# Regrouping the matmul stages of a retention and adapter kernel by the shape of the TensorE array

## The chip, the cores and the metric

The kernel runs on one core of a Trainium2 chip. The metric is the device time of one execution in microseconds; before the change it is the median of seven runs.

## What is computed

```python
B, H, S, D_ = q.shape                      # 8, 8, 576, 64, float32
scores = scale * np.matmul(q, k.transpose(0, 1, 3, 2))
gamma = 1.0 - 2.0 ** (-5.0 - np.arange(H))
Dmat = np.where(rel >= 0, gamma[:, None, None] ** rel[None, :, :], 0.0)
x = np.matmul(scores * Dmat[None], v)      # retention, per batch and head
x = x.transpose(0, 2, 1, 3).reshape(B * S, H * D_)     # 4608 x 512
logits = x @ w_gate                        # 8 experts
topk = np.argpartition(-logits, 2, axis=1)[:, :2]
w = softmax of the two chosen logits
out = x + sum over the two chosen e of w * ((x @ A[e]) @ B[e])     # A: 512x16, B: 16x512
```

The first half is a causal attention without softmax, with a decay by head. The second routes each of the 4608 rows to two of eight low-rank adapters.

## The kernel before, in words

**Units.** The sequence of 576 is cut into four chunks of 128 and one of 64. A unit is one chunk of two batches. A quad is the four batches (two units) that are loaded together; there are two quads in a chunk. So units 0 to 15 are full (unit t has chunk t // 4), and 16 and 17 are half units, which hold 64 positions of four batches each. A state P for every unit of a chunk (t % 4) carries what earlier chunks contribute; chunk 0 has none.

**Stages.** Every unit passes the stages below. In brackets stands the array shape, rows*columns, that its matmuls take in a full unit, as the profile prints it.

- T: q and k are transposed on TensorE, 16 transposes for each of qT and kT [64*128], and copied from PSUM to SBUF, by ScalarE or VectorE (two copies each, `g` = 0 and 1).
- S: scores, for batch 0 and then batch 1 (the halves `bs`) [64*128]; VectorE multiplies by the decay mask on the way out (`rt`, two for each half; `rh` in half units).
- Q: what the state contributes, written to `px` [64*64]. Chunk 0 takes the banks and issues nothing.
- U: the state's update, from k scaled by decay and v [128*64]. `scale_k` (GpSimd, line 261) scales k in place after k has been transposed and before U. VectorE adds (`pn`), GpSimd multiplies (line 395).
- R: scores times v, accumulated on `px` [128*64]; VectorE makes `xT` of each batch.
- Z: logits and the adapters' first product from `xT` [128*128] into `pz`; VectorE takes the two largest logits. V is ScalarE's sigmoid for the weights; W, on VectorE, makes the weighted `zc` and gives up the bank of `pz`.
- B: `xT` is transposed back into `po` [64*128], two banks.
- X: `zc` is transposed [128*128], ScalarE copies it to `zT`.
- Y: the adapters' second product is accumulated on `po` [128*128]; `po` is copied to `osb` by ScalarE, or with `spread` half by VectorE, and SP issues two output DMAs.

Half units take 64*64 for S, Q and R.

**What sets the order.** The order of stages is written out by hand (lines 608 to 708). `mm`, `vec` and `act` (lines 80 to 87) chain every instruction of an engine behind the one before, so each engine executes strictly in the order of the text; all their instructions show lines 81, 84 and 87 in the profile, and are told apart by the names of tiles. SP, too, issues its DMAs in the order of the text: `issue(n)` loads q, k and v of quad n, two quads ahead, into one of three buffers, and waits until that buffer has been read.

**PSUM.** `bank` (line 102) takes the first of a list of the eight banks and `done` (line 109) puts banks back at its end. This list is worked through while the program is built. On the chip, the first matmul into a bank waits for whoever last read it.

```python
    def bank(shape, name, dtype=FP32):
        n = free.pop(0)
        x = pp.tile(shape, dtype, tag=f"bank{n}", name=name)
        held[id(x)] = n, x
        return x
    def done(*tiles):
        free.extend(held.pop(id(x))[0] for x in tiles)
```

T and each half of S take two banks and put them back at once, in the list; B takes two and Y puts them back; Q takes two and R puts them back; Z takes one and W puts it back; U and X take one.

**The steady order** for a full unit t (lines 668 to 684): S(t, half 0), V(t-1), T(t+1, qT), S(t, half 1), W(t-1), T(t+1, kT), B(t-1), Q(t), U(t), scale_k(t+1), R(t), X(t-1), Z(t), Y(t-1). Each unit thus passes the four shapes once. Units 0 to 3 and the last three stand in orders of their own. Before unit 15's U, the Q of unit 16 is done too.

## Time and profile before

| | |
|---|---|
| median of seven runs | 195.27 us (193.52 to 195.41) |
| the profiled execution | 195.21 us |
| its span, first to last instruction | 193.5 us |
| TensorE clock granted, mean | 0.992 |
| ScalarE busy | 72.0 us (37%) |
| GpSimd busy | 59.0 us (31%) |
| HBM read, written | 28.91 MB, 9.44 MB |

Busy time of an engine is a union of its instructions. Matmuls are pipelined: one that is shown with 0.27 us may be followed by another 0.05 us later, so the start of a group and the start of the next tell how long it held TensorE, and its busy time does not. The profile's part 2 cuts the span into 40 slices of 4.84 us, with a digit for the busy tenths. In a timeline a line is a group of like instructions: start, busy time, engine, line, operation, tile written and tiles read, array shape for TensorE, shape of the operand, number, and in brackets the idle time before it with what ended it.

### The profile page before, as it was taken

The numbers are of one execution on the slowest core, as the hardware profiler recorded it, in microseconds if no ns is written. First come the engines' busy times: TensorE is split into PE (matmuls) and PEld (weight loads), VectorE is DVE, ScalarE is ACT, GpSimd is POOL, SyncE is SP. The second block draws the span as 40 slices with busy tenths as digits, with TensorE's granted clock in tenths as the row PEclk, the third lists the DMA queues.
The fourth block names the chain that finished last, engine by engine and source line by source line (L and its number), as shares of the span: only waits on it lengthen the run. The fifth ranks groups of instructions, "written<-read, shape, count | busy, mean of one in ns | idle before, by whom it ended". The sixth has DMA issues, their size and how long they took to land. (4 is left out here: it accounts for less than half of the span.)

```text
span 193.5 us, 8113 instructions
## 1 busy us (share of the span) xinstructions
PE 181.5 (94%) x3612; PEld 163.8 (85%) x3612; DVE 110.4 (57%) x281; ACT 72.0 (37%) x195; POOL 59.0 (31%) x70
## 2 busy tenths in 40 slices
PE   7899997999999999999998999999999999988870
PEld 2499997989999899999997999999999999977750
DVE  4467956575656474746564464646464746453650
ACT  4111164262526070707060525343444434070440
POOL 8985026040424233242415050514242420200000
PEclk9999999999999999999999999999999999999996
DMA  6999898797888598899869848999970302020243
GB/s 143 272 224 256 240 267 236 223 311 221 238 278 278 157 283 303 223 251 362 241 192 282 266 156 247 311 223 246 205 196 0 114 3 112 3 112 3 112 108 108
DMA packets 53746, 38.73 MB, mean 200 GB/s; under 512 B 27472, under 2 KB 49104, under 8 KB 53712
## 3 DMA queue, kind: packets, MB, share of 16 engines
q1 hardware_dynamic: 52736, 37.75, 69.4%
q8 instruction: 28, 0.46, 0.9%
q10 hardware_dynamic: 832, 0.34, 0.7%
q0 software_dynamic: 144, 0.13, 0.4%
q14 instruction: 6, 0.05, 0.1%
HBM read 28.91 MB, written 9.44 MB: 198 GB/s over the span
## 5 line engine op out<-in xcount | busy, mean ns | idle before, releaser
L261 POOL TENSOR_TENSOR k<-k,pack 128x512 f32<-128x512 f32 x32 | 32.7, 1042 | 81.2 <-PE pkT L81 70.6
L84 DVE TENSOR_TENSOR rt<-ps,mask 128x512 f32<-128x512 f32 x64 | 41.0, 686 | 16.5 <-PE ps L81 15.9
L81 PE MATMUL pz<-AW,xT 128*128 128x136 f32 x288 | 37.7, 283 | 0.3 <-DVE xT L84 0.2
L81 PE MATMUL ps<-qT,kT 64*128 64x128 f32 x512 | 35.7, 281 | 0.9 <-DVE kT L84 0.9
L81 PEld LDWEIGHTS pz<-AW,xT 128*128 128x128 f32 x288 | 34.7, 190 | 0.9 <-DVE xT L84 0.5
L81 PEld LDWEIGHTS ps<-qT,kT 64*128 64x128 f32 x512 | 31.0, 188 | 4.0 <-PE po L81 2.7
L81 PE MATMUL px<-rt,v 128*64 128x128 f32 x512 | 31.1, 273 | 0.7 <-issue 0.7
L87 ACT COPY osb<-po 128x256 f32<-128x256 f32 x68 | 20.6, 386 | 28.7 <-PE po L81 26.6
L84 DVE TENSOR_TENSOR xT<-px,asc 128x512 f32<-128x512 f32 x36 | 24.6, 691 | 9.0 <-PE px L81 8.0
L81 PEld LDWEIGHTS px<-rt,v 128*64 128x64 f32 x512 | 28.0, 137 | 0.8 <-issue 0.8
L87 ACT COPY zT<-pzt 128x256 f16<-128x256 f16 (+1 forms) x19 | 6.9, 361 | 53.9 <-PE pzt L81 53.9
L87 ACT COPY kT<-pkT 128x512 f32<-128x512 f32 x33 | 17.9, 590 | 14.7 <-PE pkT L81 14.7
L395 POOL TENSOR_TENSOR P<-pn,gdec 128x512 f32<-128x512 f32 x12 | 15.3, 1273 | 25.5 <-DVE pn L84 22.6
L87 ACT COPY qT<-pqT 128x512 f32<-128x512 f32 x32 | 17.2, 590 | 8.3 <-PE pqT L81 8.3
L81 PE MATMUL pu<-v,k 128*64 128x64 f32 x512 | 18.4, 225 | 1.6 <-POOL k L261 1.1
L81 PEld LDWEIGHTS pu<-v,k 128*64 128x64 f32 x512 | 16.3, 138 | 4.1 <-issue 2.6
L84 DVE COPY lg<-pz 128x16 f32<-128x16 f32 (+1 forms) x19 | 3.3, 173 | 26.4 <-PE pz L81 26.4
L84 DVE TENSOR_TENSOR pn<-pu,P 128x512 f32<-128x512 f32 x12 | 8.3, 692 | 16.0 <-PE pu L81 16.0
L81 PE MATMUL px<-qT,P 64*64 64x128 f32 (+1 forms) x512 | 15.9, 262 | 0.8 <-issue 0.7
L81 PEld LDWEIGHTS px<-qT,P 64*64 64x64 f32 x512 | 12.7, 133 | 1.8 <-issue 0.9
L81 PE MATMUL po<-id,xT 64*128 64x64 f32 x288 | 12.6, 224 | 0.7 <-DVE zc L84 0.7
L81 PE MATMUL pkT<-id,k 64*128 64x64 f32 x288 | 12.3, 223 | 0.1
(51 smaller groups left out, 150.8 us busy)
## 6 DMA issues: line engine op xcount, KB each, us to landing
out_dram<-osb SPq DMA_DIRECT2D x32, 256.0 KB, 3.1
q<-in_q_dram SPq DMA_DIRECT2D x4, 512.0 KB, 6.4
k<-in_k_dram SPq DMA_DIRECT2D x4, 512.0 KB, 7.1
v<-in_v_dram SPq DMA_DIRECT2D x4, 512.0 KB, 7.1
out_dram<-osb SPq DMA_DIRECT2D x6, 128.0 KB, 2.3
Arow<-in_moe_A_dram SPq DMA_DIRECT2D x1, 256.0 KB, 5.3
out_dram<-osb ACTq DMA_DIRECT2D x2, 128.0 KB, 2.7
Bcat<-in_moe_B_dram POOLq DMA_DIRECT2D x1, 128.0 KB, 5.1
```

The source lines that it names most:

```text
L81: chain("pe", nc.tensor.matmul(*args, **kw))
L84: chain("dve", getattr(nc.vector, fn)(**kw))
L87: chain("act", getattr(nc.scalar, fn)(**kw))
L261: gp.tensor_tensor(out=kk[:, b], in0=kk[:, b], in1=gv[:, 0].unsqueeze(2).broadcast_to((128, H, Dh)), op=ALU.mult,)
L395: nc.gpsimd.tensor_tensor(out=Pt, in0=pn, in1=gdec, op=ALU.mult)
```

## The change

The order of the stages is written anew. From unit 4 on, two units of a quad go through a loop together, and a stage of the one stands beside the same stage of the other. In the loop for t and t+1 the units of the quad before (t-2, t-1) pass Z, V and W, and those of the quad before that (t-4, t-3) pass B, X and Y. Six such loops (t = 4, 6, ... 14) are followed by a part written out for the half units. In the first part, units 2 and 3 pass S, U and R together.

With it go these edits:

- `stage_T` has a parameter `shared`; where it is set, the `g` = 1 copy is VectorE's. For unit 0 kT is copied batch by batch.
- `xT` has eight buffers instead of six, `zc` four instead of three.
- In chunk 0 U stands before Q, so U takes its bank first.
- V(1) stands before Y(0).
- Units 16 and 17 are transposed inside the loop of t = 14, between Q and U.

```diff
+    def stage_T(t, names=("qT", "kT"), shared=False):
...
+                if t == 0 and nm == "kT":
+                    for b in range(2):
+                        x = dst[:, b, :, rows(g)]
+                        if g == 1:
+                            vec("tensor_copy", out=x, in_=ps[g][:, :, b])
+                        else:
+                            act("copy", out=x, in_=ps[g][:, :, b])
+                elif t < 2 and nm == "qT" or shared and g == 1:
                     vec("tensor_copy", out=o, in_=ps[g])
                 else:
                     act("copy", out=o, in_=ps[g])
...
+            stage_U(0)
             stage_Q(0)
             stage_R(0)
             stage_T(1, ("qT",))
+            stage_T(1, ("kT",), shared=True)
             scale_k(1)
             stage_Z(0)
             stage_S(1)
             stage_W(0)
+            stage_U(1)
             stage_Q(1)
             stage_R(1)
             stage_T(2, ("qT",))
             stage_B(0)
             stage_X(0)
             stage_Z(1)
+            stage_V(1)
             stage_Y(0, spread=True)
+            stage_T(2, ("kT",), shared=True)
+            stage_T(3)
             scale_k(2)
+            scale_k(3)
+            stage_S(2)
+            stage_W(1)
+            stage_S(3)
+            for u in (2, 3):
+                stage_U(u)
+                stage_Q(u)
+                stage_R(u)
...
+        if t < 4 or units[t][2] or not is_full(t):
             continue
+        done_, near = [u for u in (t - 4, t - 3) if u > 0], (t - 2, t - 1)
+        here = (t, t + 1)
+        for nm in ("kT", "qT"):
+            stage_T(t, (nm,), shared=True)
+        scale_k(t)
+        for u in done_:
+            stage_B(u)
+        stage_T(t + 1, ("kT",))
+        scale_k(t + 1)
+        stage_S(t, (0,))
+        stage_T(t + 1, ("qT",))
+        stage_S(t, (1,))
+        stage_S(t + 1)
+        for u in done_:
+            stage_X(u)
+        stage_Z(near[0])
+        stage_V(near[0])
+        for u in done_:
+            stage_Y(u)
+        stage_Z(near[1])
+        stage_V(near[1])
+        if units[t][0] > 0:
+            for u in here:
+                stage_Q(u)
+        for u in near:
+            stage_W(u)
+        if t + 2 == NU - 2:
+            stage_T(t + 2)
+            stage_T(t + 3)
+        for u in here:
+            stage_U(u)
+            if units[t][0] == 0:
+                stage_Q(u)
+            stage_R(u)
+    h, n = NU - 2, NU - 1
+    stage_S(h); stage_Q(h); stage_B(h - 4); stage_B(h - 3); stage_X(h - 4); stage_X(h - 3)
+    stage_Z(h - 2); stage_V(h - 2); stage_Y(h - 4, spread=True); stage_Y(h - 3, spread=True)
+    stage_W(h - 2); stage_S(n); stage_R(h); stage_Z(h - 1); stage_V(h - 1); stage_Q(n)
+    stage_W(h - 1); stage_B(h - 2); stage_B(h - 1); stage_X(h - 2); stage_X(h - 1)
+    stage_Z(h); stage_V(h); stage_Y(h - 2, spread=True); stage_Y(h - 1, spread=True)
+    stage_R(n); stage_W(h); stage_B(h); stage_X(h)
+    for g in range(2):
+        stage_Z(n, (g,)); stage_W(n, (g,))
+    stage_Y(h); stage_B(n)
+    for g in range(2):
+        stage_X(n, (g,)); stage_Y(n, (g,), spread=True, last=True)
```

(The last part has one call on each line in the file; it is set closer here.)

## The prediction, before the result was known

> **What bounds the kernel now.** I read the page's shares first, then its slices, then the timeline of one unit in the steady part.

> ```profile
> PE 181.5 (94%) x3612; PEld 163.8 (85%) x3612; DVE 110.4 (57%) x281; ACT 72.0 (37%) x195; POOL 59.0 (31%) x70
> ...
> PE   7899997999999999999998999999999999988870
> ```

> TensorE is full from slice 7 to slice 34; VectorE, the next engine, is busy 57% of the span. So what TensorE does between 30 and 170 us is the time, and a new wait there costs its full length.

> The timeline of TensorE (start, busy, tile, array shape rows*columns); I read starts only, from group to group:

> ```profile
> 130.97 0.65 PE L81 MATMUL pkT<-id,k 64*128 64x64 f32 x16
> 131.46 0.67 PE L81 MATMUL po<-id,xT 64*128 64x64 f32 x16
> 132.06 1.10 PE L81 MATMUL px<-qT,P 64*64 64x128 f32 x32
> 133.09 1.15 PE L81 MATMUL pu<-v,k 128*64 128x64 f32 x32
> 134.07 1.92 PE L81 MATMUL px<-rt,v 128*64 128x128 f32 x32
> 135.93 0.29 PE L81 MATMUL pzt<-ident,zc 128*128 128x128 f16 x2
> 136.05 2.07 PE L81 MATMUL pz<-AW,xT 128*128 128x136 f32 x16
> 137.96 0.60 PE L81 MATMUL po<-Bcat,zT 128*128 128x256 f16 x4
> 138.49 1.16 PE L81 MATMUL ps<-qT,kT 64*128 64x128 f32 x16
> 139.48 0.66 PE L81 MATMUL pqT<-id,q 64*128 64x64 f32 x16
> 139.98 1.11 PE L81 MATMUL ps<-qT,kT 64*128 64x128 f32 x16
> 140.93 0.65 PE L81 MATMUL pkT<-id,k 64*128 64x64 f32 x16
> ```

> One unit takes 9.95 us (139.98 is 9.95 behind the same half of S one unit before, at 130.03), with four changes of shape (64*128, 64*64, 128*64, 128*128) and no wait.

> **Price of a change of shape.** Sixteen transposes take 0.49 us with the same shape behind them (130.97 to 131.46) and 0.60 with another behind (131.46 to 132.06): +0.11. In the head, sixteen that come after a change take 0.55 (27.24 to 27.79), the next sixteen 0.50:

> ```profile
> 27.24 0.71 PE L81 MATMUL pkT<-id,k 64*128 64x64 f32 x16
> 27.79 0.67 PE L81 MATMUL pqT<-id,q 64*128 64x64 f32 x16
> 28.29 0.66 PE L81 MATMUL po<-id,xT 64*128 64x64 f32 x16
> ```

> +0.05, so 0.16 for a change. The timeline has 76 changes; I count 51 in the new order (13 in the head, 4 in each of five loops, 5 in loop t=14, 13 in the tail). 25 x 0.16 = 4.0 us gained; bounds 2.7 (the 0.11 alone) and 5.0 (0.2, an estimate a quarter above). A loop of two units without waits, by the pitch of the matmul starts inside each group: transposes 4 x 0.49, B 2 x 0.50, S 4 x 0.89, and 0.1 where S follows transposes; X, Z, Y 2 x (0.12 + 1.86 + 0.44); Q 2 x 0.88; U and R 2 x (0.93 + 1.74): 18.6, with four changes 19.2, against 2 x 9.95 = 19.9: 0.7 gained.
> [...]

> **The new wait.** In the new loop `stage_B` of both older units takes four banks before the S halves and `stage_Y` gives them back after. Four of eight remain, handed out first in first out, two at a time. Call them A, B, C, D: kT(t) takes AB, qT(t) CD, kT(t+1) AB, S(t,0) CD, qT(t+1) AB, S(t,1) CD, S(t+1,0) AB, S(t+1,1) CD, then X takes A and B, and the first Z takes C. In the kernel of now the loop holds fewer, seven are in turn, and no S waits. The evictions, from VectorE's timeline and, after the dots, from that of all engines in the tail:

> ```profile
> 139.68 1.29 DVE L84 TENSOR_TENSOR rt<-ps,mask 128x512 f32<-128x512 f32 x2 [0.88 <-PE ps L81]
> 141.12 1.29 DVE L84 TENSOR_TENSOR rt<-ps,mask 128x512 f32<-128x512 f32 x2 [0.15 <-PE ps L81]
> ...
> 170.82 1.29 DVE L84 TENSOR_TENSOR rh<-pe,maskh 128x512 f32<-128x512 f32 x2 [0.90 <-PE pe L81]
> ...
> 171.57 0.57 PEld L81 LDWEIGHTS pkT<-id,k 64*128 64x128 f32 x15 [0.23 <-DVE rh L84]
> ```

> The last pair shows such a wait in the kernel of now: transposes held 0.23 us until VectorE had read the bank (first rh ends 170.82 + 0.69 = 171.51, release 0.06). An S half is 0.89 us of TensorE and 1.29 of VectorE; VectorE starts 1.14 after S starts (139.98 to 141.12), 1.09 when the weights were loaded during a wait.
> From the start of S(t,0) at 0: rt until 1.14 + 1.29 = 2.43. S(t,1) could start at 0.95 + 0.49 = 1.44, but waits for CD until 2.49. qT(t+1) too waits 0.4 for ScalarE's kT copies (1.82 from T's start to both copies' end: 140.93 for kT, 1.07 of ScalarE from 141.67, and a release), within the same time. S(t,1)'s rt: 3.58 to 4.87. S(t+1,0) runs 3.39 to 4.28 (its qT copies end at 3.27), rt 4.78 to 6.07. S(t+1,1) waits for CD until 4.93, rt 6.02 to 7.31. X runs at 5.9 to 6.1, Z waits for C: 6.02 + 0.69 + 0.06 = 6.77. TensorE's own work up to there is 0.95 + 0.49 + 3 x 0.89 + 0.24 and a change 0.1: 4.4. So **2.4 us lost in a loop**, 0.7 gained: loop 21.6 us against 19.9.
> Bounds: a wait can't be less than nothing, so 0 below; above 2.9, when each of the three restarts costs 0.16 more, as a change of shape does. I take 2.4, worked from the nearest rows.
> [...]

> **Other parts.** *Loop t=4* has only unit 1 in B, so six banks rotate: S(5,0) waits 0.5 for qT(5). *xT to 8, zc to 4 buffers*: nothing; without them R would wait for B. *kT and qT of the first unit half on VectorE* (`shared`): ready 2.1 after the loop starts, S at 2.55, hidden; ScalarE alone would be at 2.9. *scale_k in pairs*: 4.1 us of POOL from 0.8 after loop start, U comes 16 us after; hidden. *Loads*: `issue` stands before the outputs on SP as before; k of quad 2, issued 28.8 and 10.3 to landing, is there at 39.1, wanted at 38.7, but S(4,0) waits longer for VectorE. An output buffer (of 3) is used again over 20 us later; its output lands 3.1 after issue, behind at most 9 of loads.
> *Head*: the batchwise kT copy lets S(0) begin after a 0.42 copy (osb row of VectorE) instead of 0.69: 9.53 becomes 9.25. The order is unchanged up to kT(2), 26.9. Then sigmoid(1), 0.52, stands before osb and kT on ScalarE: S(2) 29.1, S(3) 31.3 (kT(3) behind qT(3) on ScalarE), U(2) 33.2, R(3) ends 38.7. The waits before U(2) (1.1, POOL) and U(3) (0.47) go. But VectorE has rt(2), W(1), rt(3) until 36.0, then P, xT, P, xT until 39.8, kT(4), qT(4) until 41.2: S(4,0) at 41.25, 0.5 late. With 0.5 for S(5,0), t=4 ends at 57.85.
> *Loops 6 to 12*: 4 x 21.6 = 86.3, to 144.2. *Loop 14*: 16 and 17 are transposed between Q and U, on two bank pairs, and all copies are ScalarE's, 1.07 a name, 1.82 from a transpose's start: U comes 3.65 later, where the work is 2.0; 25.2 us, to 169.4.
> *Tail*: work from the rows: the half stages S, Q, R six times 0.98, B 6 x 0.50, X 6 x 0.12, Z 4 x 1.86, Y 6 x 0.44: 19.7. 13 changes: 2.1. Waits: Z(14) for zT(12) 0.5; S(17) for the osb copy of unit 12, which stands behind sigmoid(14), 1.1; Z(16) 0.6; X(16) for zc(16), behind four osb copies and xT(17) on VectorE, 1.8; the last X to Y pairs 1.3 (now gaps of 0.96 and 0.59 where 0.12 is the pitch). 27.1 us, last matmul 196.5.

> **Sum.** Now the last matmul group is at 188.5, span 193.5; 4.9 follow: span 201.4. The profiled execution took 195.21, 1.75 outside the span (median of seven: 195.27, the same). 203.1. The trace of now has two idle stretches of TensorE put down to "issue" of 0.8 to 1.0 us, which no step of mine removes; some of that falls into my waits, I carry 0.9. **204.0 us, slower by 4.5%.**

> **Rivals.**
> *The banks do not bind* (other side). If six banks rotated, as in t=4, a loop would wait 0.5 or less. It decides where the loss is below the 0.7 gained: Z would have to start by 5.1 instead of 6.77, two pairs of evictions at 0.5 instead of 1.29. Then 5 x 2.4 + 1.7 is not paid: 204.0 - 13.7 = 190.3. For: 57% VectorE; against: four banks by count, and evictions slower than S. 0.15.
> *Half a wait*: if only VectorE's pace counts and no round trip, Z comes at 1.14 + 6 x 0.60 + 0.69 + 0.06 = 5.5: 1.3 less a loop, 197.6. 0.12. (0.60 is the pitch in the rows of four rt in 2.49 us.)
> *Changes of shape are free*: the 0.16 is a wait of another kind, and the regrouping does not do what it says: 208.0. With *outputs behind three loads on SP* (9 us of issue) holding the three osb buffers in some loops, up to 212. 0.08 together, of it 0.03 above 209.

> **Numbers.** 204.0 at 0.65; with the rivals' 0.15, 0.12 and 0.08 that is 1. The forecast's own spread is 199.5 to 208.5 (1 for the changes of shape, 2.5 for the loops' waits, 2 in the tail, not all at once). The range, 195.5 to 209, leaves out the first rival, 0.15, the low edge of the second, 0.02, and the top, 0.03. A measurement here can't tell less than 0.5% from no change, so faster means below 194.3: the first rival, 0.15; within, the second's low edge: 0.02; slower: 0.83.

> **What would show it.** Right: in a steady loop, TensorE idle before ps released by rt, about 1.0 and 0.65 us, and before the first pz 0.7; loops of 21.6 us; sixteen transposes at 0.49 but at the borders. Wrong: loops near 19.2, no idle time before ps, S halves back to back. The tail is my least certain term: X of unit 16 waiting for zc.

## The result, and the profile after

The changed kernel takes 203.39 us (median of 12 runs, 202.26 to 205.17) against 195.02 for the kernel before (31 runs beside it). The ratio is 1.045, 95% interval 1.0416 to 1.0484: slower by 4.5%. The profiled execution took 204.79 us with a span of 203.1 us; the forecast was 204.0. So the median lies 0.6 below the forecast and the profiled execution 0.8 above it. TensorE's granted clock was 0.990 against 0.992, so the 9.6 us more of span are not a matter of clock.

The shares of the engines, and TensorE's row of slices (now 5.08 us each):

```profile
PE 183.7 (90%) x3612; PEld 166.7 (82%) x3612; DVE 119.2 (59%) x302; ACT 62.3 (31%) x176; POOL 58.8 (29%) x70
...
PE   7898999799999999999899999999999989989750
```

The number of matmuls is the same, TensorE's busy time is about the same (matmuls that stall one behind the other count as busy: below, 48 of them with 2.67 us of work show 4.09), and the row still reads 9 nearly everywhere. The row does not show the loss: a wait of half a microsecond in a slice of five is a 9. VectorE, at 59%, is still far from full. So the next view is the timeline of TensorE in one steady loop (start, busy, tile, shape, number):

```profile
58.65 0.71 PE L81 MATMUL pkT<-id,k 64*128 64x64 f32 x16
...
61.20 1.11 PE L81 MATMUL ps<-qT,kT 64*128 64x128 f32 x16
...
62.58 0.71 PE L81 MATMUL pqT<-id,q 64*128 64x64 f32 x15 [0.22 <-ACT kT L87]
63.10 4.09 PE L81 MATMUL ps<-qT,kT 64*128 64x128 f32 x48
67.12 0.40 PE L81 MATMUL pzt<-ident,zc 128*128 128x128 f16 x4
67.82 2.12 PE L81 MATMUL pz<-AW,xT 128*128 128x136 f32 x16 [0.31 <-DVE rt L84]
...
80.02 0.71 PE L81 MATMUL pkT<-id,k 64*128 64x64 f32 x16
```

Three halves of S, 48 matmuls, take 4.02 us (63.10 to 67.12) where 3 x 0.89 = 2.67 is the work. They show as one busy group, since each single gap is short, and that is how such a loss hides. The timeline of all engines in the same stretch opens it, by the weight loads (PEld) and VectorE's `rt`:

```profile
62.35 1.29 DVE L84 TENSOR_TENSOR rt<-ps,mask 128x512 f32<-128x512 f32 x2 [1.63 <-PE ps L81]
...
63.70 2.03 PEld L81 LDWEIGHTS ps<-qT,kT 64*128 64x128 f32 x32 [0.31 <-DVE rt L84]
...
64.68 3.68 DVE L84 TENSOR_TENSOR rt<-ps,mask 128x512 f32<-128x512 f32 x6 [1.04 <-PE ps L81]
66.03 0.96 PEld L81 LDWEIGHTS ps<-qT,kT 64*128 64x128 f32 x14 [0.30 <-DVE rt L84]
```

The first `rt` pair ends at 62.35 + 1.29 = 63.64, and the second half of S gets going at 63.70: one release, 0.06, behind it. Two of its 16 matmuls come earlier, at 63.10 and 63.31, into the bank that the first `rt` of the pair had read by 63.04; the other fourteen follow when the second has read its bank. The same happens before 66.03. The starts in the table below are those of the fourteen. Over the whole run the waits view (us in total, times, longest) has, among others:

```profile
PEld ps L81 <- DVE rt L84: 3.0, 10, 0.3
...
PEld pz L81 <- DVE rt L84: 2.4, 5, 0.5
...
PE pkT L81 <- DMA k<-in_k_dram: 1.8, 2, 1.1
PEld pqT L81 <- ACT kT L87: 1.8, 5, 0.4
```

Ten waits of S for `rt`, five of Z, five of qT(t+1): two, one and one in each of five loops, at the places that the prediction gave. None of the first two lines is in the kernel before. The waits for k are not among those that the prediction charged.

| | predicted | measured |
|---|---|---|
| S(t,0) to S(t,1) | 2.49 | 2.49 (61.205 to 63.696) |
| S(t,0) to S(t+1,0) | 3.39 | 3.38 (64.58) |
| S(t,0) to S(t+1,1) | 4.93 | 4.82 (66.03) |
| S(t,0) to the first Z | 6.77 | 6.62 (67.82) |
| one loop | 21.6 | 21.37 (58.65 to 80.02) |
| loop t=4 ends | 57.85 | 58.65 |
| loops 6 to 12 end | 144.2 | 145.39 |
| loop t=14 | 25.2 | 25.05 |
| tail, to the last matmul group | 27.1 | 27.0 |
| behind the last matmul group | 4.9 | 5.6 |

Two halves of S in the middle of that stretch, S(t,1) and S(t+1,0), follow each other with no gap: only those that come back to a bank pair too early wait.

### The profile page after: what moved, and what is told of

Read it like the earlier page. It is cut to its first block, busy times and chain, and to the rows that moved or that the text cites. A ratio compares the mean times of both kernels' runs of the same rounds, so it can differ in the third digit from the quotient of the medians.

```text
span 203.1 us, 8133 instructions
## 1 busy us (share of the span) xinstructions
PE 183.7 (90%) x3612; PEld 166.7 (82%) x3612; DVE 119.2 (59%) x302; ACT 62.3 (31%) x176; POOL 58.8 (29%) x70
## 5 line engine op out<-in xcount | busy, mean ns | idle before, releaser
L84 DVE TENSOR_TENSOR rt<-ps,mask 128x512 f32<-128x512 f32 x64 | 39.8, 684 | 17.9 <-PE ps L81 17.9
L400 POOL TENSOR_TENSOR P<-pn,gdec 128x512 f32<-128x512 f32 x12 | 15.3, 1278 | 89.5 <-DVE pn L84 88.1
L81 PE MATMUL pz<-AW,xT 128*128 128x136 f32 x288 | 37.4, 283 | 2.2 <-DVE rt L84 1.5
L81 PE MATMUL ps<-qT,kT 64*128 64x128 f32 x512 | 37.4, 282 | 2.1 <-DVE kT L84 0.6
L81 PEld LDWEIGHTS pz<-AW,xT 128*128 128x128 f32 x288 | 34.6, 190 | 3.7 <-DVE rt L84 2.4
L81 PEld LDWEIGHTS ps<-qT,kT 64*128 64x128 f32 x512 | 32.8, 188 | 4.6 <-DVE rt L84 3.0
L87 ACT COPY kT<-pkT 128x512 f32<-128x512 f32 (+1 forms) x28 | 15.1, 580 | 58.6 <-PE pkT L81 49.1
L81 PE MATMUL px<-rt,v 128*64 128x128 f32 x512 | 30.8, 273 | 0.0
L81 PEld LDWEIGHTS px<-rt,v 128*64 128x64 f32 x512 | 27.8, 137 | 0.0
L84 DVE TENSOR_TENSOR xT<-px,asc 128x512 f32<-128x512 f32 x36 | 24.4, 689 | 4.2 <-PE px L81 3.0
L84 DVE COPY lg<-pz 128x16 f32<-128x16 f32 (+1 forms) x19 | 3.3, 173 | 32.9 <-PE pz L81 32.9
L81 PE MATMUL pu<-v,k 128*64 128x64 f32 x512 | 18.4, 224 | 1.1 <-issue 1.0
L81 PEld LDWEIGHTS pu<-v,k 128*64 128x64 f32 x512 | 16.8, 138 | 2.5 <-issue 2.2
L87 ACT ACTIVATE sg<-lg,ns 128x8 f32<-128x8 f32 x36 | 9.0, 294 | 32.2 <-DVE ns L84 31.8
L87 ACT COPY osb<-po 128x256 f32<-128x256 f32 x60 | 17.4, 386 | 1.0 <-PE po L81 0.6
L87 ACT COPY qT<-pqT 128x512 f32<-128x512 f32 x26 | 14.3, 590 | 10.4 <-PE pqT L81 10.3
L84 DVE TENSOR_TENSOR pn<-pu,P 128x512 f32<-128x512 f32 x12 | 8.3, 692 | 13.2 <-PE pu L81 13.2
L81 PE MATMUL pqT<-id,q 64*128 64x64 f32 x288 | 13.9, 226 | 1.5 <-ACT kT L87 1.0
L87 ACT COPY zT<-pzt 128x256 f16<-128x256 f16 (+1 forms) x19 | 6.2, 366 | 28.8 <-PE pzt L81 28.8
L81 PE MATMUL pkT<-id,k 64*128 64x64 f32 x288 | 13.0, 226 | 2.1 <-DMA k<-in_k_dram 1.8
L81 PEld LDWEIGHTS pkT<-id,k 64*128 64x128 f32 x288 | 10.8, 139 | 4.3 <-issue 3.0
```

What stands on the lines that cost most here:

```text
L81: chain("pe", nc.tensor.matmul(*args, **kw))
L84: chain("dve", getattr(nc.vector, fn)(**kw))
L87: chain("act", getattr(nc.scalar, fn)(**kw))
L400: nc.gpsimd.tensor_tensor(out=Pt, in0=pn, in1=gdec, op=ALU.mult)
```

## The experiments

**Theory.** Both B hold four of eight banks through S; the four that are left come round faster than VectorE empties them (1.29 us for an `rt` pair, 0.89 for a half of S), and TensorE waits 2.2 to 2.4 us in a loop. The fewer changes of shape give back 0.7. **Rival.** VectorE's pace alone is the bound: four `rt` pairs stand close together in the new order, whatever the banks. A second question is the price of a change of shape, a third what the small parts are worth.

### e1 and e2: both B, or one, behind S

```diff
-        for u in done_:
-            stage_B(u)
         stage_T(t + 1, ("kT",))
 ...
         stage_S(t + 1)
+        for u in done_:
+            stage_B(u)
```

In e2 only `done_[1:]` moves behind S, and six banks are left in S.

> The changed kernel with B of both older units moved behind the four S halves, so that eight banks instead of four are in turn while S runs; number of instructions and of shape changes stay. Bank theory: no S half waits for a bank any more; what is left in a loop is 0.6 us before S(t,0) (kT and qT copies, no longer covered by B) and 0.5 us before S(t+1,0) (qT copies), so a loop of 20.3 us instead of 21.4, and about 198 us in all. Rival (VectorE is late with its ten copies in this phase, whatever banks there are): S waits as before and loses B's cover as well, loop 21.4 to 21.9, total 203 to 206.

> The changed kernel with B of the first older unit where it was and B of the second behind the S halves: six banks in turn. Bank theory: S(t,1) finds a free bank, S(t+1,0) waits 0.5 us for qT, the first Z waits 0.4 us for its bank: loop 20.3 us, about 198 us in all. Rival (VectorE's pace): as for the changed kernel, 203.

Measured, e1: 201.01 us, ratio to the kernel before 1.0346 (1.0313 to 1.038). e2: 198.23 us, 1.0235 (1.0179 to 1.029), as the bank theory expected and 5 us below the rival's 203. Loops without an idle stretch put down to "issue" take 20.42 in e1 and 20.39 in e2, where 20.3 was expected and 21.37 is the changed kernel's. TensorE in e2, in a steady loop:

```profile
103.98 2.06 PE L81 MATMUL ps<-qT,kT 64*128 64x128 f32 x32 [0.24 <-ACT qT L87]
...
107.11 2.12 PE L81 MATMUL pz<-AW,xT 128*128 128x136 f32 x16 [0.25 <-DVE rt L84]
```

The waits of S for `rt` are gone, what is left is a wait for ScalarE's qT and a shorter one of Z. So the banks held make the waits. In e1 all eight are free, and the loop is no better: without B behind the transposes, S(t,0) waits 0.49 for the copy of qT. The expected total of e1, 198, was missed by 3, and the trace accounts for a part of it: the loops from t=6 on gained 1.0 each as expected, but T(4) started 0.7 later than in the changed kernel (40.36), and loop t=4 took 19.36 us instead of 19.00. The rest stays open.

### e3: what a change of shape costs

The kernel before, with kT(t+1) transposed between U and R, in 13 units: two changes more each, no other work.

```diff
-            stage_T(t + 1, ("kT",))
             stage_B(t - 1)
             stage_Q(t)
 ...
             stage_U(t)
+            stage_T(t + 1, ("kT",))
             scale_k(t + 1)
             stage_R(t)
```

> The kernel before with kT(t+1) transposed between U and R instead of before B: in each of 13 loops two more changes of array shape, the same instructions. If a change costs 0.16 us: 13 x 0.32 = 4.2 us more, 199.2 us against 195.0. [...] If changes of shape are free: 195.0.

Measured: 198.16 us, ratio 1.0218 (1.0171 to 1.0264). A unit, from its first half of S to the next unit's:

```profile
129.62 1.16 PE L81 MATMUL ps<-qT,kT 64*128 64x128 f32 x16
...
139.87 1.16 PE L81 MATMUL ps<-qT,kT 64*128 64x128 f32 x16
```

10.247 us against 9.95, for two changes: 0.147 each.

### e4: every `rt` done twice

```diff
-                vec(
-                    "tensor_tensor", out=r, in0=ps[ho], in1=mask[ho], op=ALU.mult,
-                )
+                for _ in range(2):
+                    vec(
+                        "tensor_tensor", out=r, in0=ps[ho], in1=mask[ho], op=ALU.mult,
+                    )
```

> The changed kernel with each eviction of a full S half done twice by VectorE (the same product into the same tile). Bank theory: the pair of evictions that S(t,1) and S(t+1,1) and the first Z wait for takes 2.5 us instead of 1.29, the chain from S(t,0) to Z gets 4.1 us longer: loop 25.5 us instead of 21.4; with 3 in loop t=4 and 4 in the head, about 230 us. Rival (the loss is not in these waits but in the later B, X, Y and in transfers): VectorE has 38 us more work but is busy 59% of the span, so under 5 us more, 208 at most.

Measured: 254.97 us, ratio 1.3126 (1.3022 to 1.3231); loops of 28.2 to 29.8 us where 25.5 was expected. From S(t,0) to the first Z it is 11.87 us (102.03 to 113.90), expected 10.9. The sign and the place are those of the theory, the size is not. The rest is seen in busy time by stretch (stretch; length; busy and number for PE, PEld, DVE, ACT and POOL; granted clock; DMA):

```profile
104.00:106.00 2.00, 0.58 (x6) 0.29 (x2) 1.88 (x3) 1.07 (x2) 0.31 (x1) 1.00 0.97 288
106.00:108.00 2.00, 1.94 (x24) 1.97 (x26) 0.92 (x2) 0.00 (x0) 0.00 (x0) 0.72 0.65 196
108.00:110.00 2.00, 1.44 (x14) 1.18 (x10) 1.97 (x4) 0.00 (x0) 0.00 (x0) 0.50 0.01 2
...
116.00:118.00 2.00, 2.00 (x15) 1.93 (x14) 0.38 (x3) 0.00 (x0) 0.00 (x0) 0.72 0.00 0
```

In this run the granted clock falls to 0.50 in each of the five loops, for 6.8 or 10.2 us in all, and matmuls with no wait between them take twice as long (the first Z of a loop: 3.4 to 3.5 us from its first to its last matmul instead of 1.8).

### e5: the small parts alone

The kernel before with the batchwise kT copy of unit 0 and U ahead of Q in units 0 to 2.

> The kernel before with two small parts of the change alone: the first unit's kT copied batch by batch, and U ahead of Q's banks in chunk 0. By the prediction's step: S(0) begins after a copy of 0.42 us instead of 0.69, all later work follows, 0.3 us less (194.7 against 195.0), which is less than one measurement can tell. If something later absorbs it: no difference.

Measured: 194.28 against 195.02, ratio 0.9953 (0.9922 to 0.9985): a gain, of about the half per cent that can just be told. S(0) starts 1.35 behind the transposes of kT(0), instead of 1.62: the 0.27 predicted. Little more can come of it: kT(1) then waits 0.99 us for the load of k.

### e6: the same pairs, with B between the halves of S

The changed kernel with its loop written differently: T of both units, S(t), B(t-4), S(t+1), B(t-3), Z(t-2), both X, Z(t-1), both Y, then Q, W, U, R as before. No stage is added or left out, nor a change of shape in the loop.

> The changed kernel with another order inside the loops: all four transposes first, B of the one older unit between the two S and B of the other behind them, the first Z ahead of X. Same instructions, same changes of shape; ten or more matmul groups lie between an S half and the next user of its bank. Bank theory: 0.1 us left of the waits, loop 19.4 us instead of 21.4, about 193 us in all. Rival (VectorE's pace, 10 copies of 0.6 us in a phase of 7 us, decides): Z can't begin earlier than 7.7 us into the loop, loop 19.9 to 20.3, 196 to 198 us.

Measured: 195.14 us, ratio 0.9975 (0.9942 to 1.0008). TensorE in a steady loop:

```profile
117.94 0.71 PE L81 MATMUL pkT<-id,k 64*128 64x64 f32 x16
...
120.16 2.06 PE L81 MATMUL ps<-qT,kT 64*128 64x128 f32 x32
122.02 0.69 PE L81 MATMUL po<-id,xT 64*128 64x64 f32 x16
122.51 2.03 PE L81 MATMUL ps<-qT,kT 64*128 64x128 f32 x32
...
137.44 0.72 PE L81 MATMUL pkT<-id,k 64*128 64x64 f32 x16
```

No wait stands before S, B or Z. The loop is 19.50 us (117.94 to 137.44), 1.9 less than the changed kernel's and 0.3 over the 19.2 without waits; the rival's 19.9 to 20.3 is excluded. VectorE does the same eight `rt`, so its pace is no bound when B's work stands between them and eight banks go round. This is the counter-proof: without the waits the pairing does gain, 0.4 us per loop of the 0.7 that the prediction gave it, and the loss came from where B, which holds the banks, was placed. The whole is no faster than the kernel before, so the other parts cost what the loops gain.

### e11: the kernel before, with two banks set aside

```diff
+        if t == 3:
+            aside = [free.pop(0) for _ in range(2)]
+        if t == NU - 3:
+            free.extend(aside)
```

> The kernel before with two of the eight banks set aside in the loops of units 3 to 14: order, instructions and shapes stay. Bank theory: S(t, half 1) gets a bank that VectorE still reads and waits 0.35 us, B waits 0.4 us: 0.75 us in each of 12 units, 9 us more, 204 us. Rival (banks do not matter, VectorE's pace does, which is the same here): 195 us.

Measured: 210.14 us, ratio 1.0765 (1.0691 to 1.0839). Same instructions, same order, two banks less: a unit goes from 9.95 to 11.36 (118.28 less 106.92 below). VectorE's work is the same, so its pace alone can't explain this. The theory's size was too small, though: 9 us were expected and 15.3 came. It had the waits of S and B, and not those of Q's `px`, which now takes a bank that W frees late. From TensorE's timeline and, after the dots, the waits view:

```profile
106.92 1.50 PE L81 MATMUL ps<-qT,kT 64*128 64x128 f32 x15
...
118.28 1.49 PE L81 MATMUL ps<-qT,kT 64*128 64x128 f32 x15
...
PEld px L81 <- DVE zc L84: 4.8, 11, 0.4
...
PEld po L81 <- DVE rt L84: 2.6, 12, 0.2
PEld ps L81 <- DVE rt L84: 2.5, 12, 0.2
```

### e7 to e10 and e12: can the pairing pay?

With e6's loop the rest of the gain must come from the tail, where the half units pass alone. e7 takes both half units through the tail together: their four T at its start, Q, S, R and B of both side by side. e8 is the changed kernel with that tail alone.

> As e6, and the half units go through the tail together: transposes of 16 and 17 at its start, Q, S, R of both, then the B, Z, X, Y in pairs (7 to 8 changes of shape instead of 13 in the tail and 2 in loop 14). By the prediction's sums the tail with its transposes took 30.8 us up to the last matmul and takes 23.6 now: 7 us less than e6, 186 us. If the tail's length is that of its evictions and not of its waits and changes of shape: as e6, 193 us.

> The changed kernel with the tail of e7 alone, loops untouched. By the prediction's terms for loop 14 (1.7 us of waits) and for the tail (5.1 us of waits, 6 changes of shape): 7 us less, 196.4 us. If those terms are misjudged and the loops are the whole loss: 203.

Measured, e7: 195.46 us, the median of ten runs that lie between 192.27 and 197.75, so far from the 186 us expected, and no gain over the kernel before (195.02) is shown. The profile is of a run of 196.62. e8: 203.43, ratio 1.0415 (1.0354 to 1.0476), no gain over the changed kernel. The tail of e7, from T(16) to the last matmul, is 29.3 us where 23.6 was expected. TensorE there:

```profile
171.52 0.73 PE L81 MATMUL px<-qT,P 64*64 64x64 f32 x33 [1.07 <-issue]
...
175.65 1.73 PE L81 MATMUL px<-rh,v 64*64 64x64 f32 x98 [2.04 <-issue]
...
179.10 0.27 PE L81 MATMUL po<-id,xT 64*128 64x64 f32 x2 [0.64 <-issue]
```

3.75 us of idle time that the view puts down to no other engine and no transfer of data, in the middle of stages, while no tile changes. e9 mixes the short 64*64 stages with long ones (Q, S of 16; B, X, Y of 14 and 15; R(16), Q, S of 17; Z(16); R(17)). e10 is e7 without the output transfers of two units (four of 256 KB, not eight as its expectation says), in case instructions arrive by the same way.

> As e7, with the 64x64 stages of the half units no longer all in one stretch: Q, S of 16, then B, X, Y of 14 and 15, then R of 16 and Q, S of 17, then Z of 16, and R of 17 behind it. In e7's tail TensorE stood still 3.7 us for its own instruction stream (three idle stretches put down to issue, 1.07, 2.04 and 0.64 us), the long ones where 512 short instructions follow each other. If it is that stretch, a tail 3 to 4.5 us shorter than e7's: 189 to 190.5 us against 193.4 for e7. If it is the transfers that run at the time, whatever TensorE executes: as e7.

> e7 without the output transfers of units 12 and 13 (8 transfers of 256 KB are left out, all else stays), which start just before those idle stretches. If instructions reach TensorE late because they queue behind these transfers, the idle stretches of 1.07 and 2.04 us go: about 3 us less than e7. If TensorE simply executes short matmuls faster than instructions can be brought, they stay and the time is e7's.

Measured, e9: 192.32 us (191.02 to 192.86), ratio 0.987 (0.9801 to 0.9939): below both kernels, with the long idle stretches of that part gone (one of 0.40 stays), though 2 to 3 us short of what was expected: Y waits 0.96 and 0.62 for `zT` and 0.39 for `osb` at the end. e10: 194.58 us, about e7's time, and the idle stretches stay (0.77, 1.49, 1.20). Those transfers are not the cause.

Counting TensorE's instructions in the trace (matmuls, weight loads, and the few semaphore instructions) gave a pattern: the idle stretches of the tails stand 127 to 128 matmuls apart, and over all kernels, e12 with them, 29 of the 30 of at least 0.2 us lie at the 192nd or 193rd instruction of a block of 256: number 3776 and 6849 in the kernel before, 3520 in the changed one, 6593, 6849 and 7105 in e7. e12 tests it by 64 more instructions in the head of e7:

> The kernel with both units through loop and tail (e7), and 32 small matmuls more (64 instructions of TensorE with their weight loads) among the warming ones in the head; nothing else. In the runs so far nearly every idle stretch of TensorE put down to issue lies at the same place of its instruction stream, the 192nd to 194th of a block of 256, counted with weight loads and the few semaphore instructions: 3776 and 6849 in the kernel before, 3520 in the changed one, 6593, 6849 and 7105 in e7. Theory, instructions arrive in blocks of 256 and the next block is late: the idle stretches keep their number in the stream, so they move 32 matmuls forward in the stages: from within Q(17), 31 matmuls done, to S(16), 63 done; from R(16), 30 done, to S(17), 62 done; from B(17), 30 done, to R(17), with 62 of its 64 done; the one in U(7), 26 of 32 done, to the Q before it. About the same time, 193 to 196 us. Rival, the stall belongs to the stage (its state, its bank, the tile of k or v): it stays at Q(17), 31 done, R(16), 30 done and B(17), 30 done.

Measured: 193.81 us, ratio 0.996 (0.9918 to 1.0003). TensorE in the tail:

```profile
171.15 0.27 PE L81 MATMUL pe<-qT,kT 64*64 64x64 f32 x2 [2.05 <-issue]
...
175.25 0.32 PE L81 MATMUL px<-rh,v 64*64 64x64 f32 x2 [1.89 <-issue]
```

The idle stretches moved to the places named: before the last two matmuls of S(17) and before the last two of R(17), and the one in S(16), behind 63 (0.21 us). The one in U (it is unit 9's, not 7's) is not seen at all in this execution, nor is it in every other one. The stretches belong to the number in the stream and not to a stage.

The trace has the transfers too. The page of every run lists a DMA queue for instructions (packets, MB, share of 16 engines), here as before and after the change:

```profile
q8 instruction: 28, 0.46, 0.9%
```

They are 28 transfers of 16 KB (16384 bytes in the records); TensorE's 7289 instructions in the traces before and after make 28 whole blocks of 256. In the trace's records of them, each of the 29 stretches ends 1.22 to 1.52 us behind the end of one; in e7 they end at 170.23, 174.42 and 177.66, and TensorE goes on at 171.52, 175.65 and 179.10; in the changed kernel one ends at 99.33, and TensorE goes on at 100.58; in the kernel before, they end at 103.41 and 174.86, and it goes on at 104.82 and 176.23. In none of the fourteen traces does TensorE pass a 192nd place sooner than 1.22 us behind the end of its transfer. So the author puts these stretches down to waits for the next block of instructions.

## Why the prediction was right

**What bounds.** Right: TensorE's own stream is the time, and a wait in it costs its length (a loop takes 21.37 us, 2.2 over the 19.2 without waits). VectorE rose to only 59%, and still its evictions decide: it is when they come, not how many.

**The new wait.** Right in cause, place and size. The bank order A to D gave every step of the chain to 0.15 us (table above). Of the 2.4 us lost in a loop 2.2 came: S(t+1,1) comes 0.11 and Z 0.15 sooner. The 1.09 from S to its `rt` behind a wait stands in no row of before; it is an estimate (the rows have 1.19, 1.16 and 1.14 with the weight load 0, 0.03 and 0.06 ahead of S), and 0.98 (63.70 to 64.68) and 1.05 (66.03 to 67.08) were measured. e2 (four to six banks), e6 (B between the halves) and e11 (two less in the kernel before) each turn it by the banks.

**Changes of shape.** 0.16 was predicted, 0.147 measured (e3); for 25 changes 3.7 us instead of 4.0. The rival "changes of shape are free" is excluded; its 208.0 would have needed that.

**Head.** The batchwise copy gave its 0.27; S(2) came at 29.0 for 29.1 and U(2) at 32.93 for 33.2. Wrong was that k of quad 2 costs nothing: its load was issued at 30.49, not at 28.8 as in the trace before, kT(4) waits 1.1 us for it (39.65, where 38.7 was said), and S(4,0) starts at 41.91, not 41.25. This shows as the 0.8 us by which loop t=4 ends late. And kT(1) waits 0.7 for its k, which the prediction did not look at. Together these are the 1.8 us of the waits view. That the wait of kT(1) did no harm is luck: the head began 0.69 earlier in this execution than in the trace before (kT(0) at 7.22, not 7.91), so that S(0) came at 8.57, not 9.25. The change did not do that; e6, with the same head, began at 8.19, and e3, the old head, at 7.40 with a wait of 0.63 for the same k.

**Loops 6 to 12.** 86.7 us for 86.3: four times 21.37, and 1.26 that one of them took longer, for an idle stretch by "issue" in U(9) (before 100.58). The 0.9 that the prediction carried for such idle time is this.

**Loop 14 and tail.** 25.05 for 25.2 and 27.0 for 27.1. That the tail agrees to 0.1 is partly luck: X(16) waits 1.25 us for `zc`, not 1.8, and the last Y waits 1.46 and 0.51 for `zT`, some 0.7 more than assumed.

**Rivals.** "The banks do not bind" decides at a loss of 0.7 us in a loop; the loss was 2.2. "Half a wait" had Z at 5.5 behind S; it came at 6.62. Both fall with one number of the timeline. Nor does any copy into `osb` wait for a transfer in the waits view, so outputs behind three loads on SP cost nothing here.

**The total.** The terms are right to some 0.2 us in each loop, loop 14 and the tail; the 0.8 us of loop t=4 and 0.7 behind the last matmul group, which the prediction took over from the trace before, are what it missed. The twelve runs lie up to 2.9 us apart, so that the median falls within 0.6 of the forecast is in part luck.

## What to carry to other kernels

When stages are regrouped, write down which PSUM banks go round in the new order and let the list turn by hand: with starts from the trace and the time of an eviction, it gave each wait to 0.15 us before anything was built. Keep a stage that holds banks (here B) out of the stretch in which banks turn fastest, or put it between the evictions, as in e6: the same work, 1.9 us less per loop. A saving on TensorE's stream brings up what arrives just in time: here the load of k for kT(4) (1.1 us of wait), and in the tails of e7 and e8 the instructions themselves (idle stretches of 3.75 and 3.79 us in all).

## What the runs showed of the hardware that was not expected

**The granted clock was 0.50 for some microseconds in the middle of a run.** In e4 TensorE was busy 0.58 of 2.0 us (104 to 106), its longest single idle stretch there was 0.86 us, and soon after the clock was 0.50 for 10.2 us (106.86 to 117.10). In e12, behind idle stretches of 2.05 and 1.89 us, it was 0.50 for 3.4 us, and Z took 3.62 us instead of 2.1. In the changed kernel, busy 5.87 of 6.60 us from 61.2 to 67.8, it stayed at 1.00. Between its changes within e4 lie whole multiples of 3.41 us (106.86 to 117.10 is three). In the last 3.41 us ahead of a fall TensorE was busy 1.93 us in e4 (103.45 to 106.86) and 1.52 in e12 (173.05 to 176.46). But e8 kept the full clock with 1.80 and 1.91 of 3.40 us (176.1 to 179.5 to 182.9), so no limit comes out of these runs.
